# A fused attention-reading and expert kernel: the fourth batch's G is read inside its own unit, and raw second-layer weights are asked for in steps 10 to 12

## The chip, the core and the metric

The kernel runs on one core of one Trainium2 chip. The metric is the device time of one execution in microseconds, the median over runs. Engines are named as in the profile: PE is TensorE's matrix multiplication, PEld its weight load, DVE is VectorE, ACT is ScalarE, POOL is GpSimd, and SP is the engine that here only issues DMAs.

## The reference

```python
# x: B=4, H=8, S=512, D=64;  state: B, H, Ns=32, D
xread = softmax(scale * x @ state.T) @ state          # B,H,512,64
sread = softmax(scale * state @ x.T) @ x              # B,H,32,64
t = concat([xread, sread], axis=2) -> tokens 2176 x 512

P = exp(t @ w_gate - max)                             # 2176 x 8 experts
8 times: P /= row sums; P /= column sums; P *= N / E
y = sum over e of P[:, e] * (relu(t @ w1[e]) @ w2[e]) # w1 512x1024, w2 1024x512

h = y @ w_in                                          # 512 x 2048
out = (h * sigmoid(h)) @ w_out                        # 2048 x 512
```

## The kernel before

Every fp32 product is made of three fp32r products. A tile is split into a high part (a copy rounded to fp32r) and a low part (the rest), and `mm3` (L83 to L86) issues low times high on L84, high times low on L85 and high times high on L86.

The first expert layer is not computed from the tokens as they are. A token's xread is a mixture `a` of rows of `state`, so t @ w1 is a @ (state · w1), and the product of state and w1, called G, is made once per unit for all four batches. A unit is one half of one expert's hidden width: 8 experts times 2 halves are 16 units, u = 0 to 15. The G of a unit is computed one unit ahead in two pieces (`g_pieces`, matmuls pg on L441, ACT's copies and DVE's subtractions into `stg`), written to a DRAM tile `g_d` (L448) and read back batch by batch by `load_g(u, b)`, four DMAs on L475 each, in the layout the matmuls want.

A unit is 16 steps, k = 4 b + f: four batches b of 512 tokens, and four chunks f of 128 hidden columns. In a step PE runs S1 of the step that lies two ahead (6 matmuls into the bank `ph`; then ACT's relu `hh` on L512 and DVE's low part `hl` on L513), and then S2 of the step itself (12 matmuls into four banks `po`, with the step's `hh`, `hl` as one operand and the second-layer weights of chunk f, `h_w` and `l_w`, as the other). At a batch's last chunk DVE adds P times the four banks to `acc` (L567). PE keeps the order in which the code is written. The order on the other engines and on SP's queue is set by a scheduler when the kernel is built, from the order of the code and its own estimate of when data comes; each engine then works through its list in that order.

A weight tile takes four steps. SP asks for the raw tile (L182, `raw_w` in the trace, `raw_w2_7_0` in the order for unit 7, chunk 0). ACT casts it to the high part (L190, `h_w`), DVE subtracts to get the low part (L89, `l_w`), and PE uses both. The raw tiles share a pool with the tag "raw", three buffers deep before. The w2 pool holds five split tiles, one more than a unit needs: so chunk 0 of the next unit has a free slot, and chunk f = 1, 2, 3 of it needs the slot that S2 of step 12 + f − 1 frees. S2 of the new unit needs chunk f at its own step f, five steps later.

The calls in the main loop that belong to the change: for most units `load_w1(u + 2, ·)` at steps 7 to 10, `load_g(u + 1, b)` at steps 8, 9, 11 and 14 (units 0 and 1: 12 to 15), `load_w2(u + 1, f)` at steps 12 to 15, after the calls of `load_g`. Between them `convert` prepares the weights of the second network (raw64, cv, cvo; DMAs of wi_d and wo_d issued by ACT). After the 16 units the second network runs with the same S1 and S2 over w_in and w_out; it uses the "raw" buffers for `gv` and the tag "e2" for `sg`. In the first unit, steps also carry pieces of the attention stage, in a table `early`: ahead of S2 its first list, behind S2 its second; `positions(b)` makes softmax weights (tile `e2`), `back(b)` works on from there.

Of the kernel before, what the change touches and what calls it, by code (L numbers as in the profile page):

```python
# [11 lines left out]
F32 = mybir.dt.float32  # L12
# [9 lines left out]
def fused_kernel(ctx: ExitStack, tc: tile.TileContext, x, state, w_gate, w1, w2, w_in, w_out, out):  # L22
# [18 lines left out]
    DM = H * D  # L41
    E, _, F = w1.shape
# [18 lines left out]
    stp = ctx.enter_context(tc.tile_pool(name="stp", bufs=4))  # L61
    accp = ctx.enter_context(tc.tile_pool(name="accp", bufs=4))
    wp = ctx.enter_context(tc.tile_pool(name="wp", bufs=5))
    rawp = ctx.enter_context(tc.tile_pool(name="rawp", bufs=3))
    hp_ = ctx.enter_context(tc.tile_pool(name="hp", bufs=4))
    srp = ctx.enter_context(tc.tile_pool(name="srp", bufs=1))
    att = ctx.enter_context(tc.tile_pool(name="att", bufs=5))
# [116 lines left out]
    def load_split(src_ap, shape, nm, tag, slots, engine=nc.vector):  # L184
        if nm not in raws:
            load_raw(src_ap, shape, nm)
        raw = raws.pop(nm)
        hi = wp.tile(shape, F32R, tag=tag + "h", name=f"h_{nm}", bufs=slots)
        lo = wp.tile(shape, F32R, tag=tag + "l", name=f"l_{nm}", bufs=slots)
        nc.scalar.copy(hi, raw)  # L190
        lo_of(lo, raw, hi, engine)
        return hi, lo
# [8 lines left out]
        else:  # L201
            w1t[u, hp] = load_split(src, [128, FU], f"w1_{u}_{hp}", "w1", 4, nc.gpsimd if u == 0 else nc.vector)

    def load_w2(u, f):
        e, fh = divmod(u, UPE)
        r0 = fh * FU + f * 128
        w2t[u, f] = load_split(w2[e, r0:r0 + 128, :], [128, DM], f"w2_{u}_{f}", "w2", 5)

# [118 lines left out]
    def positions(b, q):  # L329

        pq = pm(f"pq{b}_{q}")
        for r in range(R):
            nc.tensor.transpose(pq[:, r * 128:(r + 1) * 128], s1_of[b][:, r, q * 128:(q + 1) * 128], ident)
        e2 = e2_of[b, q] = att.tile([128, 512], F32, tag="e2", name=f"e2_{b}_{q}", bufs=4)
        nc.scalar.copy(e2, pq)
        m2 = sm.tile([128, 1], F32, tag="m2", name=f"m2_{b}_{q}")
        nc.vector.tensor_reduce(out=m2, in_=e2, axis=AX.X, op=ALU.max)
        nc.vector.tensor_scalar_mul(m2, m2, -scale)
        z2 = sm.tile([128, 1], F32, tag="z2", name=f"z2_{b}_{q}")
        nc.scalar.activation(out=e2, in_=e2, func=AF.Exp, scale=scale, bias=m2, accum_out=z2)  # L340
        nc.vector.tensor_scalar_add(z2, z2, 1e-9)
        nc.vector.reciprocal(out=z2, in_=z2)
        nc.vector.tensor_scalar_mul(e2, e2, z2)
# [135 lines left out]
    def sr_first(u):  # L479
        ps = p1(f"psr_{u}")  # L480
        for hp in range(KD):
            wh, wl = w1t[u, hp]
            mm3(ps, srh[:, hp], srl[:, hp], wh, wl, hp == 0, hp == KD - 1)
        t = att.tile([128, FU], F32, tag="e2", name=f"hs_{u}", bufs=4)
        nc.scalar.activation(out=t, in_=ps, func=AF.Relu)
        hS[u] = t

# [14 lines left out]
    def S1(u, b, f):  # L502
        ph = p1(f"ph{u}_{b}_{f}")
        if u < NU:
            gh, gl = G[u, b][:, :, 0], G[u, b][:, :, 1]
            ah, al = (t[:, b % 2] for t in aT[b // 2])
            fs = slice(f * 128, (f + 1) * 128)
            for q in range(2):
                mm3(ph, gh[:, q, fs], gl[:, q, fs], ah[:, q], al[:, q], q == 0, q == 1)
            hh = hp_.tile([128, 512], F32R, tag="hh", name=f"hh{u}_{b}_{f}")  # L510
            hl = hp_.tile([128, 512], F32R, tag="hl", name=f"hl{u}_{b}_{f}")
            nc.scalar.activation(out=hh, in_=ph, func=AF.Relu)  # L512
            last["dve"] = nc.vector.scalar_tensor_tensor(out=hl, in0=ph, scalar=0.0, in1=hh.bitcast(F32), op0=ALU.max, op1=ALU.subtract)  # L513
        else:
            wh, wl = wit[u - NU, f]
            n = 128 * len(chunks[b])
            for k in range(KD):
                xh, xl = x2[b, k]
                mm3(ph[:, :n], wh[:, k], wl[:, k], xh, xl, k == 0, k == KD - 1)
            sg = att.tile([128, 512], F32, tag="e2", name=f"sg{u}_{b}_{f}", bufs=4)  # L520
            nc.scalar.activation(out=sg[:, :n], in_=ph[:, :n], func=AF.Sigmoid)  # L521
            gv = rawp.tile([128, 512], F32, tag="raw", name=f"gv{u}_{b}_{f}")
            nc.vector.tensor_tensor(out=gv[:, :n], in0=ph[:, :n], in1=sg[:, :n], op=ALU.mult)  # L523
            hh = hp_.tile([128, 512], F32R, tag="hh", name=f"hh{u}_{b}_{f}")
            hl = hp_.tile([128, 512], F32R, tag="hl", name=f"hl{u}_{b}_{f}")
            nc.scalar.copy(hh[:, :n], gv[:, :n])
            lo_of(hl[:, :n], gv[:, :n], hh[:, :n])
        hT[u, b, f] = (hh, hl)
# [74 lines left out]
    def both(piece, b, *bank):  # L603
# [4 lines left out]
        -1: ([lambda: x_turn(2, 2, pm), lambda: x_turn(2, 3, pm)], []),  # L608
        0: (both(scores, 2, pm) + [lambda: slots(2, 1)], both(mixing, 1, pm)),
        1: (both(positions, 0), [lambda hp=hp: x_turn(3, hp, pm) for hp in range(KD)]),  # L610
        2: (both(positions, 1), both(back, 0) + both(scores, 3, pm) + [lambda: slots(3, 1), lambda: state_reads(0)]),
        3: (both(mixing, 2, pm), [lambda: g_first(1, 0)]),
        4: ([lambda: g_first(1, 1)], [lambda: g_first(1, 2)]),
        5: ([lambda: g_first(1, 3)], both(back, 1)),
# [58 lines left out]
    for i in range(-LAG, len(steps)):  # L673
# [19 lines left out]
        if u < NU:  # L693
            if 0 < u:
                if u == 1 and k == 2:
                    sr_first(1)
                if u == 1 and k == 4:
                    sr_turn(1)
                if k == 7:
                    sread_second(u)  # L700
                if u + 1 < NU:
                    if k == (11 if u == 1 else 6):
                        sr_first(u + 1)
                    if k == (13 if u == 1 else 9):
                        sr_turn(u + 1)
                if u + 1 >= NU and k < 4:
                    load_win(0, k)
                convert_some((u - 2) * B * NF + k + 5)
            for unit, hp in first.get(u, {}).get(k, ()):
                load_w1(unit, hp)  # L710
            at = 12 if u == 1 else 7
            if 1 <= u and u + 2 < NU and at <= k < at + 4:
                load_w1(u + 2, k - at)
            loads = (12, 13, 14, 15) if u <= 1 else (8, 9, 11, 14)
            if u + 1 < NU and k in loads:
                load_g(u + 1, loads.index(k))
            if k >= 12:
                load_w2(u + 1, k - 12) if u + 1 < NU else load_wout(0, k - 12)
            if u == NU - 1:
                if 6 <= k < 10:  # L720
                    turn(0, k - 6)
                if 10 <= k < 14:
                    turn(1, k - 10)
                if k >= 14:
                    turn(2, 2 * (k - 14))
                    turn(2, 2 * (k - 14) + 1)
        else:
            v = u - NU
            if v == 0 and k < 8:
                turn(3 + k // 4, k % 4)  # L730
            if v + 1 < NV:
                if b == 3 and f < 2:
                    load_win(v + 1, f)
                if b == 4:
                    if f < 2:
                        load_win(v + 1, f + 2)
                    load_wout(v + 1, f)
# [31 lines left out]
```

## Time and profile before

| | before |
|---|---|
| median of 3 runs | 1740.56 us (1738.30 to 1741.57) |
| profiled execution, its own time | 1744.39 us |
| span of the profiled execution | 1742.6 us |
| mean granted TensorE clock | 0.988 |
| PE busy | 1690.5 us, 97% of the span |
| PEld, DVE, ACT busy | 1396.2, 891.2, 492.3 us |

The time of an execution is a little longer than the span, which runs from its first to its last instruction. The profiled execution lies 3.83 us above the median of the runs. The granted clock is the share of TensorE's full rate (2.4 GHz) that it was given, so 0.50 means 1.2 GHz.

### The profile page before, as it was taken

Reading aid. Unit: us, or ns where it says so; the run is one execution under the profiler, and the core shown is the slowest. Engines: PE = TensorE matmul, PEld = TensorE weight load, DVE = VectorE, ACT = ScalarE, POOL = GpSimd, SP = SyncE. Lnnn points to the kernel's source line nnn. Section 1 sums busy time; section 2 is a strip of 40 time slices with the busy share of each in tenths; the row PEclk is TensorE's granted clock in tenths of the full one; section 3 lists DMA queues with packets and bytes.
Section 4 is the critical chain, followed back from the end, with each engine's and each line's share of the span. In section 5 each row is a group of like instructions: output and inputs, shape, how many; then the busy total and the mean of one; then the engine's idle time right before and its main releaser. Section 6 shows DMA issues by size and latency. Waiting matters only on the chain.

```text
span 1742.6 us, 20238 instructions
## 1 busy us (share of the span) xinstructions
PE 1690.5 (97%) x7868; PEld 1396.2 (80%) x7868; DVE 891.2 (51%) x1524; ACT 492.3 (28%) x891; POOL 12.6 (1%) x15
## 2 busy tenths in 40 slices
PE   8999999999999999999999999999999999999999
PEld 7878787877878787878778787878788888888888
DVE  7642575555555555565655655465434433433333
ACT  5642244222222222232322222232212322222222
POOL 1010000000000000000000000000000000000000
PEclk9989999999999999999999999999999999999999
DMA  7042376565745464655647465655540103020211
GB/s 170 19 150 70 96 201 199 132 205 146 195 160 164 138 176 165 167 185 136 206 145 206 139 167 171 170 183 125 169 109 7 43 1 97 1 97 1 85 49 55
DMA packets 107631, 222.07 MB, mean 127 GB/s; under 512 B 28560, under 2 KB 44944, under 8 KB 107536
## 3 DMA queue, kind: packets, MB, share of 16 engines
q1 hardware_dynamic: 101152, 201.76, 40.5%
q10 hardware_dynamic: 6384, 19.02, 2.8%
q8 instruction: 62, 1.02, 0.2%
q14 instruction: 33, 0.27, 0.0%
HBM read 136.59 MB, written 84.15 MB: 127 GB/s over the span
## 4 chain that ended last, share of the span: by engine, by line
PE 79%; DVE 2%; issue 1%; ACT 1%; ACTq 0%; DVEq 0%
PE po L85 16%; PE po L84 15%; PE po L86 15%; PE ph L86 9%; PE ph L84 9%; PE ph L85 9%; PE pg L441 3%; DVE acc L567 1%; PE psr L85 1%; PE psr L84 1%; PE psr L86 1%; DVE l_w L89 1%; ACT hh L512 1%; PE px L591 0%; DVE hl L513 0%
## 5 line engine op out<-in xcount | busy, mean ns | idle before, releaser
L84 PE MATMUL po<-h_w,hl 128*128 128x512 f32 x1024 | 410.4, 401 | 22.7 <-ACT h_w L190 22.7
L85 PE MATMUL po<-l_w,hh 128*128 128x512 f32 x1024 | 406.6, 397 | 14.1 <-DVE l_w L89 14.1
L86 PE MATMUL po<-h_w,hh 128*128 128x512 f32 x1024 | 404.0, 395 | 0.0
L513 DVE SCALAR_TENSOR_TENSOR hl<-ph,hh 128x512 fp32r<-128x512 f32 x256 | 176.7, 690 | 419.8 <-ACT hh L512 419.3
L512 ACT ACTIVATE hh<-ph 128x512 fp32r<-128x512 f32 x256 | 153.2, 598 | 666.0 <-PE ph L86 662.2
L84 PEld LDWEIGHTS po<-h_w,hl 128*128 128x128 f32 x1024 | 194.7, 190 | 79.6 <-ACT h_w L190 29.8
L85 PEld LDWEIGHTS po<-l_w,hh 128*128 128x128 f32 x1024 | 195.0, 190 | 61.3 <-DVE l_w L89 22.5
L86 PEld LDWEIGHTS po<-h_w,hh 128*128 128x128 f32 x1024 | 195.1, 191 | 40.8
L84 PE MATMUL ph<-aTh,G 128*128 128x512 f32 x512 | 203.5, 398 | 0.4 <-DVE hl L513 0.4
L86 PE MATMUL ph<-aTh,G 128*128 128x512 f32 x512 | 200.2, 391 | 0.0
L85 PE MATMUL ph<-aTl,G 128*128 128x512 f32 x512 | 200.2, 391 | 0.0
L567 DVE SCALAR_TENSOR_TENSOR acc<-po,P,acc 128x512 f32<-128x512 f32 x224 | 153.1, 742 | 6.6 <-PE po L86 6.6
L523 DVE TENSOR_TENSOR gv<-ph,sg 128x384 f32<-128x384 f32 (+1 forms) x80 | 48.9, 611 | 191.2 <-ACT sg L521 191.2
L84 PE MATMUL ph<-x2h,wil 128*128 128x384 f32 (+1 forms) x320 | 115.4, 361 | 0.0
L86 PE MATMUL ph<-x2h,wih 128*128 128x384 f32 (+1 forms) x320 | 114.7, 358 | 0.0
L85 PE MATMUL ph<-x2l,wih 128*128 128x384 f32 (+1 forms) x320 | 114.4, 357 | 0.0
L86 PEld LDWEIGHTS ph<-aTh,G 128*128 128x128 f32 x512 | 96.5, 189 | 20.6
L84 PEld LDWEIGHTS ph<-aTh,G 128*128 128x128 f32 x512 | 96.9, 189 | 19.8 <-DVE hl L513 0.6
L85 PEld LDWEIGHTS ph<-aTl,G 128*128 128x128 f32 x512 | 96.8, 189 | 19.1
L86 PE MATMUL po<-woh,hh 128*128 128x512 f32 x272 | 106.8, 393 | 0.0
L85 PE MATMUL po<-wol,hh 128*128 128x512 f32 x272 | 106.7, 392 | 0.0
L84 PE MATMUL po<-woh,hl 128*128 128x512 f32 x272 | 105.8, 389 | 0.0
(163 smaller groups left out, 1848.9 us busy)
## 6 DMA issues: line engine op xcount, KB each, us to landing
g_d<-stg SPq DMA_DIRECT2D x120, 512.0 KB, 4.0
G<-g_d SPq DMA_DIRECT2D x240, 256.0 KB, 5.5
raw_w<-in_moe_w_dram SPq DMA_DIRECT2D x136, 256.0 KB, 5.3
raw<-in_moe_w_in_dram SPq DMA_DIRECT2D x16, 512.0 KB, 6.2
wi_d<-cvo ACTq DMA_DIRECT2D x16, 512.0 KB, 2.7
raw<-in_moe_w_out_dram SPq DMA_DIRECT2D x16, 512.0 KB, 6.3
wo_d<-cvo ACTq DMA_DIRECT2D x16, 512.0 KB, 3.1
x<-in_x_dram SPq DMA_DIRECT2D x16, 256.0 KB, 4.9
```

The lines of the kernel that those rows point to most:

```text
L84: nc.tensor.matmul(ps, al, bh, start=first, stop=False)
L85: nc.tensor.matmul(ps, ah, bl, start=False, stop=False)
L86: nc.tensor.matmul(ps, ah, bh, start=False, stop=last)
L89: engine.tensor_tensor(out=lo, in0=src, in1=hi.bitcast(F32), op=ALU.subtract)
L441: nc.tensor.matmul(pg[hp, half], a[lanes[half], hp], w[lanes[half]], start=i == 0, stop=i == 2)
L512: nc.scalar.activation(out=hh, in_=ph, func=AF.Relu)
L513: last["dve"] = nc.vector.scalar_tensor_tensor(out=hl, in0=ph, scalar=0.0, in1=hh.bitcast(F32), op0=ALU.max, op1=ALU.subtract)
L523: nc.vector.tensor_tensor(out=gv[:, :n], in0=ph[:, :n], in1=sg[:, :n], op=ALU.mult)
L567: nc.vector.scalar_tensor_tensor(out=a, in0=ps, scalar=P[:, t, e:e + 1], in1=a, op0=ALU.mult, op1=ALU.add)
```

## The change

The raw pool gets a fourth buffer, and the tag "e2" has three in place of four. `load_w2` can ask for the raw tile alone. For units 1 to 14 the raw tiles of the next unit's w2 are asked for in step 10 (chunk 0), 11 (chunks 1 and 2) and 12 (chunk 3); the cast and the subtraction are still called in steps 12 to 15, and now ahead of the calls for w1 and G. The read of G's fourth batch moves out of the unit before into step 0 of the unit that uses it, and the third batch's from step 11 to step 12 (unit 0 and 1: from 14 to 15). In step 2 of the first unit `back(0)` and `positions(1)` change places.

```diff
-    rawp = ctx.enter_context(tc.tile_pool(name="rawp", bufs=3))
+    rawp = ctx.enter_context(tc.tile_pool(name="rawp", bufs=4))
...
-    def load_w2(u, f):
+    def load_w2(u, f, only_raw=False):
...
+        if only_raw:
+            load_raw(w2[e, r0:r0 + 128, :], [128, DM], f"w2_{u}_{f}")
+        else:
+            w2t[u, f] = load_split(w2[e, r0:r0 + 128, :], [128, DM], f"w2_{u}_{f}", "w2", 5)
...
# e2, hs and sg, all with the tag "e2":  bufs=4  ->  bufs=3
...
-        2: (both(positions, 1), both(back, 0) + both(scores, 3, pm) + [lambda: slots(3, 1), lambda: state_reads(0)]),
+        2: (both(back, 0), both(positions, 1) + both(scores, 3, pm) + [lambda: slots(3, 1), lambda: state_reads(0)]),
...
+            if k >= 12:
+                load_w2(u + 1, k - 12) if u + 1 < NU else load_wout(0, k - 12)
             for unit, hp in first.get(u, {}).get(k, ()):
                 load_w1(unit, hp)
             at = 12 if u == 1 else 7
             if 1 <= u and u + 2 < NU and at <= k < at + 4:
                 load_w1(u + 2, k - at)
-            loads = (12, 13, 14, 15) if u <= 1 else (8, 9, 11, 14)
+
+            if u and k == 0:
+                load_g(u, 3)
+            for f in ({10: (0,), 11: (1, 2), 12: (3,)}.get(k, ()) if 1 <= u and u + 1 < NU else ()):
+                load_w2(u + 1, f, True)
+            loads = (12, 13, 15) if u <= 1 else (8, 9, 12)
             if u + 1 < NU and k in loads:
                 load_g(u + 1, loads.index(k))
-            if k >= 12:
-                load_w2(u + 1, k - 12) if u + 1 < NU else load_wout(0, k - 12)
```

What the scheduler makes of it is seen best where unit 7 follows unit 6; the other boundaries look alike. ACT's list before, from the first cast of unit 7's w2 (`h_w2_7_f`) on; `hh7_0_2` is the relu of unit 7, batch 0, chunk 2, and `ph7_0_2` its bank:

```order
L190 CAST h_w2_7_0_5358<-raw_w2_7_0_5356 128x512
L512 ACTIVATE hh7_0_2_5472<-ph7_0_2_5465 128x512
L190 CAST h_w2_7_1_5389<-raw_w2_7_1_5387 128x512
L244 DMA wo_d1_167<-cvo_13_5456 128x1024
L512 ACTIVATE hh7_0_3_5500<-ph7_0_3_5493 128x512
L446 CAST stg8_0_0_5527<-pg8_0_0_5511 128x512
L446 CAST stg8_0_1_5531<-pg8_0_1_5512 128x512
L446 CAST stg8_1_0_5535<-pg8_1_0_5519 128x512
L446 CAST stg8_1_1_5539<-pg8_1_1_5520 128x512
L512 ACTIVATE hh7_1_0_5562<-ph7_1_0_5555 128x512
L190 CAST h_w2_7_2_5424<-raw_w2_7_2_5422 128x512
L190 CAST h_w2_7_3_5461<-raw_w2_7_3_5459 128x512
```

The same place in ACT's list after, from the relu of unit 6's batch 3, chunk 2 on:

```order
L515 ACTIVATE hh6_3_2_5336<-ph6_3_2_5329 128x512
L190 CAST h_w2_7_0_5357<-raw_w2_7_0_5295 128x512
L190 CAST h_w2_7_1_5393<-raw_w2_7_1_5325 128x512
L515 ACTIVATE hh6_3_3_5375<-ph6_3_3_5368 128x512
L244 CAST cvo_13_5453<-cv_13_5287 128x512
L190 CAST h_w2_7_2_5421<-raw_w2_7_2_5327 128x512
L515 ACTIVATE hh7_0_0_5404<-ph7_0_0_5397 128x512
L190 CAST h_w2_7_3_5456<-raw_w2_7_3_5361 128x512
L515 ACTIVATE hh7_0_1_5432<-ph7_0_1_5425 128x512
L515 ACTIVATE hh7_0_2_5467<-ph7_0_2_5460 128x512
L247 DMA wo_d1_167<-cvo_13_5453 128x1024
L515 ACTIVATE hh7_0_3_5500<-ph7_0_3_5493 128x512
```

The casts of chunks 0 and 1 move from behind `hh7_0_1` and `hh7_0_2` to behind `hh6_3_2`, three and four relus earlier, and those of chunks 2 and 3 from behind `hh7_1_0` to behind `cvo_13` and `hh7_0_0`, five and four relus earlier. DVE's subtractions `l_w2_7_f` go with them: chunk 0's stands behind the four `acc` additions of unit 6's last batch before, and ahead of them after.

SP's queue before, from the read of G's first batch for unit 7 on (x4 are the four DMAs of one `load_g`):

```order
L475 DMA G_7_0_5209<-g_d7_4902 32x2x1024 x4
L475 DMA G_7_1_5255<-g_d7_4902 32x2x1024 x4
L223 DMA raw64_13_5285<-in_moe2_w_out_dram 128x1024
L182 DMA raw_w1_8_3_5289<-in_moe_w1_dram 128x512
L475 DMA G_7_2_5323<-g_d7_4902 32x2x1024 x4
L182 DMA raw_w2_7_0_5356<-in_moe_w2_dram 128x512
L182 DMA raw_w2_7_1_5387<-in_moe_w2_dram 128x512
L475 DMA G_7_3_5417<-g_d7_4902 32x2x1024 x4
L182 DMA raw_w2_7_2_5422<-in_moe_w2_dram 128x512
L182 DMA raw_w2_7_3_5459<-in_moe_w2_dram 128x512
L448 DMA g_d8_5510<-stg8_0_0_5527 128x1024
L448 DMA g_d8_5510<-stg8_0_1_5531 128x1024
```

SP's queue after, from the same place on:

```order
L478 DMA G_7_0_5209<-g_d7_4902 32x2x1024 x4
L478 DMA G_7_1_5255<-g_d7_4902 32x2x1024 x4
L226 DMA raw64_13_5285<-in_moe2_w_out_dram 128x1024
L182 DMA raw_w2_7_0_5295<-in_moe_w2_dram 128x512
L182 DMA raw_w2_7_1_5325<-in_moe_w2_dram 128x512
L182 DMA raw_w2_7_2_5327<-in_moe_w2_dram 128x512
L182 DMA raw_w2_7_3_5361<-in_moe_w2_dram 128x512
L478 DMA G_7_2_5363<-g_d7_4902 32x2x1024 x4
L478 DMA G_7_3_5488<-g_d7_4902 32x2x1024 x4
L451 DMA g_d8_5510<-stg8_0_0_5527 128x1024
L451 DMA g_d8_5510<-stg8_0_1_5531 128x1024
```

The four raw tiles of w2 now stand together ahead of the reads of `G_7_2` and `G_7_3`, and `raw_w1_8_3` has moved up out of this piece; before, `raw_w2_7_2` and `raw_w2_7_3` were queued behind `G_7_3`.

## Rows read from the trace of the kernel before

**Rows 1.** The page, part 1: busy time of each engine, its share, instructions.

```profile
PE 1690.5 (97%) x7868; PEld 1396.2 (80%) x7868; DVE 891.2 (51%) x1524; ACT 492.3 (28%) x891; POOL 12.6 (1%) x15
```

**Rows 2.** Waits of TensorE, whole span: total us, times, longest.

```profile
PE po L84 <- ACT h_w L190: 22.7, 17, 3.1
PE po L85 <- DVE l_w L89: 14.1, 22, 1.5
...
PE pq L333 <- DVE aTl L89: 1.2, 1, 1.2
```

**Rows 3.** Timeline of TensorE: the first boundary wait of all, unit 1.

```profile
184.48 0.49 PE L84 MATMUL po<-h_w,hl 128*128 128x512 f32 x1 [1.08 <-ACT h_w L190]
```

**Rows 4.** Timeline of TensorE: the last boundary wait, unit 14.

```profile
1226.37 0.50 PE L85 MATMUL po<-l_w,hh 128*128 128x512 f32 x1 [0.32 <-DVE l_w L89]
```

**Rows 5.** Timeline of TensorE where unit 7 begins.

```profile
662.47 0.39 PE L84 MATMUL po<-h_w,hl 128*128 128x512 f32 x1
663.86 0.50 PE L85 MATMUL po<-l_w,hh 128*128 128x512 f32 x1 [1.00 <-DVE l_w L89]
664.20 0.40 PE L86 MATMUL po<-h_w,hh 128*128 128x512 f32 x1
```

**Rows 6.** Timeline of TensorE, third step of unit 7.

```profile
675.26 0.49 PE L84 MATMUL po<-h_w,hl 128*128 128x512 f32 x1 [1.25 <-ACT h_w L190]
```

**Rows 7.** Timeline of ScalarE around the same boundary.

```profile
658.65 0.60 ACT L512 ACTIVATE hh<-ph 128x512 fp32r<-128x512 f32 x1 [3.48 <-PE ph L86]
659.14 0.61 ACT L190 CAST h_w<-raw_w 128x512 fp32r<-128x512 f32 x1
...
674.11 0.60 ACT L512 ACTIVATE hh<-ph 128x512 fp32r<-128x512 f32 x1 [1.76 <-PE ph L86]
674.60 1.13 ACT L190 CAST h_w<-raw_w 128x512 fp32r<-128x512 f32 x2
```

**Rows 8.** Timeline of VectorE around the same boundary.

```profile
659.28 0.69 DVE L513 SCALAR_TENSOR_TENSOR hl<-ph,hh 128x512 fp32r<-128x512 f32 x1 [3.06 <-ACT hh L512]
659.89 2.71 DVE L567 SCALAR_TENSOR_TENSOR acc<-po,P,acc 128x512 f32<-128x512 f32 x4
...
663.12 0.68 DVE L89 TENSOR_TENSOR l_w<-raw_w,h_w 128x512 fp32r<-128x512 f32 x1
```

**Rows 9.** Timeline of SP's queue ahead of unit 7 (rows may join issues).

```profile
642.92 0.83 SPq L182 DMA_DIRECT2D raw_w<-in_moe_w_dram  x2
650.42 1.74 SPq L475 DMA_DIRECT2D G<-g_d  x4
652.26 11.93 SPq L182 DMA_DIRECT2D raw_w<-in_moe_w_dram  x2
```

**Rows 10.** The tile raw_w, 620 to 670 us: issue to landing.

```profile
DMA to landing us min/median/max: 2.6/2.7/9.4
```

**Rows 11.** Five half-clock stretches: length, busy by engine, clock, DMA share, GB/s.

```profile
593.99:600.82 6.83, 6.16 (x15) 4.81 (x16) 1.21 (x3) 0.00 (x0) 0.00 (x0) 0.50 0.86 273
...
sum 20.48, PE 19.53 PEld 15.06 DVE 6.13 ACT 1.19 POOL 0.00; mean PE 3.91 PEld 3.01 DVE 1.23 ACT 0.24 POOL 0.00
```

**Rows 12.** Timeline of TensorE within the half-clock stretch of 593.99.

```profile
596.10 0.63 PE L85 MATMUL po<-l_w,hh 128*128 128x512 f32 x1
596.53 0.63 PE L86 MATMUL po<-h_w,hh 128*128 128x512 f32 x1
```

**Rows 13.** Timeline of ScalarE where unit 15 follows unit 14.

```profile
1277.88 0.62 ACT L190 CAST h_w<-raw_w 128x512 fp32r<-128x512 f32 x1 [2.12 <-PE po L86]
1279.24 0.60 ACT L512 ACTIVATE hh<-ph 128x512 fp32r<-128x512 f32 x1 [0.74 <-DVE l_w L89]
```

**Rows 14.** Timeline of TensorE at that place.

```profile
1279.04 0.39 PE L84 MATMUL po<-h_w,hl 128*128 128x512 f32 x1
...
1281.53 0.39 PE L86 MATMUL po<-h_w,hh 128*128 128x512 f32 x1
```

**Rows 15.** The page, part 6: DMA issues, KB each, median us to landing.

```profile
G<-g_d SPq DMA_DIRECT2D x240, 256.0 KB, 5.5
```

More of the change, by code (lines that the diff above doesn't have):

```diff
@@ L202, in load_w1 @@
             w1t[u, hp] = load_split(src, [128, FU], f"w1_{u}_{hp}", "w1", 4, nc.gpsimd if u == 0 else nc.vector)
-    def load_w2(u, f):
+    def load_w2(u, f, only_raw=False):
         e, fh = divmod(u, UPE)
         r0 = fh * FU + f * 128
-        w2t[u, f] = load_split(w2[e, r0:r0 + 128, :], [128, DM], f"w2_{u}_{f}", "w2", 5)
+        if only_raw:
+            load_raw(w2[e, r0:r0 + 128, :], [128, DM], f"w2_{u}_{f}")
+        else:
+            w2t[u, f] = load_split(w2[e, r0:r0 + 128, :], [128, DM], f"w2_{u}_{f}", "w2", 5)
     wi_d = [dram.tile([KD, 128, 2, FU], F32, name=f"wi_d{v}") for v in range(NV)]
@@ L333, in positions @@
             nc.tensor.transpose(pq[:, r * 128:(r + 1) * 128], s1_of[b][:, r, q * 128:(q + 1) * 128], ident)
-        e2 = e2_of[b, q] = att.tile([128, 512], F32, tag="e2", name=f"e2_{b}_{q}", bufs=4)
+        e2 = e2_of[b, q] = att.tile([128, 512], F32, tag="e2", name=f"e2_{b}_{q}", bufs=3)
         nc.scalar.copy(e2, pq)
@@ L483, in sr_first @@
             mm3(ps, srh[:, hp], srl[:, hp], wh, wl, hp == 0, hp == KD - 1)
-        t = att.tile([128, FU], F32, tag="e2", name=f"hs_{u}", bufs=4)
+        t = att.tile([128, FU], F32, tag="e2", name=f"hs_{u}", bufs=3)
         nc.scalar.activation(out=t, in_=ps, func=AF.Relu)
@@ L519, in S1 @@
                 mm3(ph[:, :n], wh[:, k], wl[:, k], xh, xl, k == 0, k == KD - 1)
-            sg = att.tile([128, 512], F32, tag="e2", name=f"sg{u}_{b}_{f}", bufs=4)
+            sg = att.tile([128, 512], F32, tag="e2", name=f"sg{u}_{b}_{f}", bufs=3)
             nc.scalar.activation(out=sg[:, :n], in_=ph[:, :n], func=AF.Sigmoid)
```

## The prediction

> **What bounds the kernel now.** I read the page's busy shares first: PE is busy for 1690.5 us, 97% of the span [rows 1]. Nothing that leaves PE's instructions as they are can win more than PE's idle time and what PE does slowly, so the next view is that of PE's waits. Two of its rows hold nearly all of the idle time after the first stage: PE waits 17 times for `h_w` (22.7 us) and 22 times for `l_w` (14.1 us), 36.8 us in 39 waits [rows 2]. In the timeline they lie between 184.48 and 1226.37 us [rows 3, 4], every one where a unit begins, at each of the units 1 to 14. So the thing to explain is one boundary, and whether its cause goes.
>
> I take the one to unit 7. PE has the high part of chunk 0 at 662.47 but waits 1.00 us for its low part [rows 5]. Of chunk 2 it lacks the high part and waits 1.25 us [rows 6]. The raw data is not the cause: SP asks for chunks 0 and 1 at 642.92 and for chunk 2 at 652.26 [rows 9], and landing takes 2.7 us in the median and 9.4 at most [rows 10], so by 661.7 chunk 2 is there, 13 us before its cast. The cause is the place in the lists. ACT casts chunk 0 only behind the relu of 658.65, though a slot is free, and chunks 2 and 3 behind the relu of 674.11 [rows 7], which itself comes from the S1 directly ahead of the S2 that wants the weights. DVE then does chunk 0's subtraction behind the `hl` of 659.28 and four additions to `acc`, and ends 3.4 us after the cast [rows 7, 8]. The read of `G_7_3` at 650.42 also holds up SP: raw chunks 2 and 3 are queued behind it [rows 9], which is a reason for the scheduler to expect them late.
>
> **What the waits cost beyond themselves.** Where nothing waits, matmuls start every 0.226 us (1279.04 to 1281.53 in 11 steps) [rows 14]. From 662.47 to 664.20 two steps take 1.73 us where 0.45 would do, so a wait of 1.00 costs 1.28 us: 0.28 more than the view of waits says [rows 5]. I give that to each of the 39: 10.9 us. Third, there are five stretches at half clock (granted 0.50, that is 1.2 GHz), all right behind boundary waits, 20.48 us with 19.53 us of PE at work [rows 11]. There a matmul starts every 0.43 us [rows 12], so 1 − 0.226 / 0.43 = 0.474 of that work, 9.3 us, is lost. By the Trainium skill (TensorE: Matmul & The Clock Gate, section Terms) the penalty is the throttled time times one minus the granted share, 20.48 × 0.5 = 10.2 us, by which the saving below would be 57.9 us. The trace's cadence decides, and the sum goes by 9.3.
>
> **The change part by part.** *Raw tiles of w2 asked for in steps 10 to 12, load_w2 called ahead of w1 and G, fourth raw buffer.* No instruction is added on PE, ACT or DVE. In the order after, the casts of unit 7 stand three to five relus earlier and the subtractions go with them, chunk 0's ahead of the four additions. A step is 18 matmuls, 4.08 us. Chunk 0 is then cast behind the relu at about 658.65 − 3 × 4.08 = 646.4, some 16 us before PE wants it. Chunks 1 to 3 each wait for their slot, and get it from the S2 five steps ahead of their own: from its end some 17 us remain for a cast of 0.61 and a subtraction of 0.69 us. The kernel before has this pattern once: at unit 15 the cast waits 2.12 us for PE, ends at 1278.50, and the relu behind it starts at 1279.24, in its usual place after S1 [rows 13], while PE runs on without a wait [rows 14]. So I take all three parts at the full size:
>
> 36.8 + 10.9 + 9.3 = 57.0 us, 4.1 us for each of the 14 boundaries.
>
> *The read of the fourth batch's G at step 0 of its own unit, the third's one step later.* The same DMAs, later. Batch 3's first S1 runs at step 10 of the unit, some 40 us behind the call, and a read takes 5.5 us to land [rows 15]. In SP's order `G_7_3` stands directly behind `G_7_2`, and waits for the same S1 as before, so it leaves near 650 as it does now [rows 9]. Cost: nothing, covered by 35 us; with that cover gone PE would stand still for up to 5.5 us at each of 15 units, 82 us.
>
> *Tag "e2" with three buffers.* `sg` is read by the next DVE operation and then free; PE has no wait after 1226.37 [rows 4], so nothing there leans on a fourth buffer. Taken at nothing. *Step 2 of unit 0.* `positions(1)` and `back(0)` change places; the largest wait of PE for such a piece is 1.2 us [rows 2]. It may go or come twice: between −1.2 and +1.2, and I take 0.
>
> **The sum.** The profiled execution would go from 1744.39 to 1687.4 us. It lies 3.83 us above the median of the runs, so the median would be 1740.56 − 57.0 = 1683.6. I leave 2 us for waits that stay, at unit 1 above all, where the calls keep steps 12 to 15 in the unit before and the casts have the least room. Forecast: 1686 us.
>
> **The rivals.**
>
> *The clock stays.* Only two of the parts return and the stretches at half clock remain, for another reason than the waits: in the one of 593.99 the DMA engines are busy at 0.86 [rows 11], so it could be them. Against it: five of the 14 boundaries have such a stretch and no place without waits has one in this part. Time: 1740.56 − 36.8 − 10.9 = 1692.9.
>
> *Half of the boundaries keep their waits*, because the raw tiles, now all behind one another, come late there or the scheduler finds no earlier place. The order speaks against it, since I find the casts moved two to five steps at each of the 14 boundaries. Time: 1740.6 − 28.5 = 1712.
>
> *The change doesn't do what it says.* The casts stand earlier in the lists, but wait there, and PE gets its weights no sooner. They would have to be some 16 us late for that. Time: about 1740.
>
> *Slower: early casts hold up the relus.* ACT works through its list in order, so a cast that waits for a raw tile holds the relus behind it, and with them `hh`, `hl` and PE. By the Trainium skill (PSUM — Partial Sum Buffer, section Engine vs sequencer instructions) the queues of ScalarE and VectorE are strictly first in, first out, which speaks against putting a cast further ahead. The trace agrees: at 1279.24 the relu starts only after the cast of 1277.88 [rows 13]. Its price: S1 writes a bank again two steps, 8.16 us, later; from S1's first matmul to the end of `hl` some 2.8 us pass (six matmuls of 0.226, then 0.60 and 0.69 [rows 7, 8]). So a relu may be 5.3 us late for nothing; each us more costs 1 us at each boundary, and the kernel becomes slower once a raw tile is some 5.3 + 4.1 = 9.4 us late at all 14. At 12 us it would be 14 × 6.7 − 57 = 37 us slower, 1777. Against it: in SP's order the four raw tiles stand ahead of `G_7_2`, whose read waits for an S1 four steps ahead of `G_7_3`'s 650.42. Even if they left only then, at 634, and took the longest landing, 9.4 us [rows 10], they would be there at 643.5, 3 us before the relu of 646.4.
>
> **How the numbers follow.** A measurement of this kernel can't tell 0.2%, 3.5 us, from no change. All three parts return: 0.74 (1680 to 1690). The clock stays: 0.10. Half of the boundaries: 0.08. No change: 0.04. Slower: 0.04. The range for 8 in 10 begins at 1678, which is the sum without the 2 us left over, less 1.2 us for step 2 and the spread of the three runs shown; it reaches up past the clock's case to 1704, where five of the boundaries keep their 4.1 us. Faster 0.92, same 0.04, slower 0.04.
>
> **What would show it.** Right: in the view of PE's waits the rows for `h_w` and `l_w` fall from 36.8 us to under 4; the mean granted clock rises from 0.988, with 0.50 only before 184 us; on ACT the casts of a unit's w2 stand behind the relus of the last batch before it, with idle time released by PE's `po`. PE's busy time would fall by what the half clock cost. The raw tiles of w2 would land before the relu that their cast follows. Wrong: waits of ACT for DMAs of `raw_w` with relus late behind them and new waits of PE for `hl`; waits of PE for `G`; or half-clock stretches where PE has no wait ahead.

## The result

| | before | changed |
|---|---|---|
| median of the first series | 1739.70 us (4 runs, 1738.30 to 1741.57) | 1680.14 us (4 runs, 1679.99 to 1690.46) |
| profiled execution, its own time | 1744.39 us | 1679.99 us |
| its span, mean granted clock | 1742.6 us, 0.988 | 1678.2 us, 1.000 |
| pooled median | 1740.10 us (36 runs beside the experiments, 1735.92 to 1747.85) | 1683.22 us (14 runs: these 4, and 10 of two later series, 1679.99 to 1690.46) |

The changed kernel is faster: the ratio is 0.9672, with a 95% interval from 0.9634 to 0.9710; the forecast of 1686 us stands at 0.969 of the first median before. Two later series, told below, gave 0.9680 both times, at 1683.18 and 1684.94 us. One more run of before, at 4316.87 us and a granted clock of 1.000, is far outside all the others and is left out of every number here.

In the page of the profile PE's busy share goes from the 97% of [rows 1] to 99%. Engine, busy us, share of the span and instructions:

```profile
PE 1660.0 (99%) x7868; PEld 1383.1 (82%) x7868; DVE 893.7 (53%) x1524; ACT 493.4 (29%) x891; POOL 12.7 (1%) x15
```

PE has the same 7868 instructions. In the view of PE's waits from 170 to 1228 us, where 39 waits for `h_w` and `l_w` took 36.8 us [rows 2], neither is left. Two other waits stand there now; such waits took 0.2 us before. In total, times, longest:

```profile
PE pc L420 <- DVE cs L417: 1.1, 1, 1.1
PE pg L444 <- DVE hl L516: 0.9, 1, 0.9
```

Unit 7 now begins at 625.48 us. TensorE's timeline there, against [rows 5]: start, us, operation.

```profile
625.48 0.39 PE L84 MATMUL po<-h_w,hl 128*128 128x512 f32 x1
625.71 0.39 PE L85 MATMUL po<-l_w,hh 128*128 128x512 f32 x1
625.94 0.39 PE L86 MATMUL po<-h_w,hh 128*128 128x512 f32 x1
```

Start follows start after 0.23 us. The same boundary on ScalarE, against [rows 7]; in brackets the idle time ahead of an instruction and what ended it:

```profile
609.42 0.60 ACT L515 ACTIVATE hh<-ph 128x512 fp32r<-128x512 f32 x1 [3.54 <-PE ph L86]
609.92 0.61 ACT L190 CAST h_w<-raw_w 128x512 fp32r<-128x512 f32 x1
612.08 0.62 ACT L190 CAST h_w<-raw_w 128x512 fp32r<-128x512 f32 x1 [1.55 <-PE po L86]
613.50 0.60 ACT L515 ACTIVATE hh<-ph 128x512 fp32r<-128x512 f32 x1 [0.80 <-PE ph L86]
616.18 0.62 ACT L244 CAST cvo<-cv 128x512 fp32r<-128x512 f32 x1 [2.08 <-DVE cv L238]
616.71 0.61 ACT L190 CAST h_w<-raw_w 128x512 fp32r<-128x512 f32 x1
617.58 0.60 ACT L515 ACTIVATE hh<-ph 128x512 fp32r<-128x512 f32 x1 [0.26 <-PE ph L86]
620.24 0.62 ACT L190 CAST h_w<-raw_w 128x512 fp32r<-128x512 f32 x1 [2.06 <-PE po L86]
621.66 0.60 ACT L515 ACTIVATE hh<-ph 128x512 fp32r<-128x512 f32 x1 [0.80 <-PE ph L86]
```

The four casts of unit 7's w2 start at 609.92, 612.08, 616.71 and 620.24, all before the unit begins. Two of them wait for PE's `po`, that is for their slot, and not for data (the prediction had such a wait for three of them); the relus of 613.50 and 621.66 behind them still wait for PE. VectorE's list there, against [rows 8]:

```profile
620.90 0.69 DVE L89 TENSOR_TENSOR l_w<-raw_w,h_w 128x512 fp32r<-128x512 f32 x1 [1.66 <-ACT h_w L190]
622.29 0.69 DVE L516 SCALAR_TENSOR_TENSOR hl<-ph,hh 128x512 fp32r<-128x512 f32 x1 [0.70 <-ACT hh L515]
622.90 2.71 DVE L570 SCALAR_TENSOR_TENSOR acc<-po,P,acc 128x512 f32<-128x512 f32 x4
```

The last subtraction of the four runs ahead of the `acc` additions of 622.90. And SP's queue, against [rows 9], where two raw tiles of w2 left at 642.92 and the others between 652.26 and 664.19; now all four leave together, ahead of the next read of G:

```profile
587.64 4.12 SPq L182 DMA_DIRECT2D raw_w<-in_moe_w_dram  x4
596.62 9.58 SPq L478 DMA_DIRECT2D G<-g_d  x2
```

### The profile page after: what moved, and what is told of

It is laid out like the page before. It is cut to its first block, busy times and chain, and to the rows that moved or that the text cites. A ratio compares the mean times of both kernels' runs of the same rounds, so it can differ in the third digit from the quotient of the medians.

```text
span 1678.2 us, 20174 instructions
## 1 busy us (share of the span) xinstructions
PE 1660.0 (99%) x7868; PEld 1383.1 (82%) x7868; DVE 893.7 (53%) x1524; ACT 493.4 (29%) x891; POOL 12.7 (1%) x15
## 4 chain that ended last, share of the span: by engine, by line
PE 84%; DVE 0%; issue 0%
PE po L84 17%; PE po L85 16%; PE po L86 16%; PE ph L84 10%; PE ph L86 10%; PE ph L85 10%; PE pg L444 3%; PE psr L85 1%; PE psr L84 1%; PE psr L86 1%; PE px L594 0%; PE pt L495 0%; DVE acc L566 0%; DVE l_w L89 0%; DVE accs L566 0%; DVE hl L516 0%
## 5 line engine op out<-in xcount | busy, mean ns | idle before, releaser
L84 PE MATMUL po<-h_w,hl 128*128 128x512 f32 x1024 | 404.2, 395 | 0.0
L86 PE MATMUL po<-h_w,hh 128*128 128x512 f32 x1024 | 398.9, 390 | 0.0
L85 PE MATMUL po<-l_w,hh 128*128 128x512 f32 x1024 | 398.8, 389 | 0.0
L84 PEld LDWEIGHTS po<-h_w,hl 128*128 128x128 f32 x1024 | 192.2, 188 | 49.4 <-issue 10.9
L89 DVE TENSOR_TENSOR l_w<-raw_w,h_w 128x512 fp32r<-128x512 f32 x128 | 87.1, 690 | 61.5 <-ACT h_w L190 60.8
L524 ACT ACTIVATE sg<-ph 128x384 f32<-128x384 f32 (+1 forms) x80 | 42.8, 535 | 220.2 <-PE ph L86 217.6
```

Of the source, the lines that this page charges most:

```text
L84: nc.tensor.matmul(ps, al, bh, start=first, stop=False)
L85: nc.tensor.matmul(ps, ah, bl, start=False, stop=False)
L86: nc.tensor.matmul(ps, ah, bh, start=False, stop=last)
L89: engine.tensor_tensor(out=lo, in0=src, in1=hi.bitcast(F32), op=ALU.subtract)
```

## Where the time came from: the granted clock read run by run

The 36 runs of the kernel before differ by 12 us, the 14 of the changed one by 10, and each run's time goes with its mean granted clock. The runs of before at 0.993 take 1735.9 to 1736.8 us, those at 0.986 take 1747.2 to 1747.9. The changed kernel's runs at 1.000 take 1680.0 to 1680.2 us, those at 0.997 take 1683.0 to 1683.5, those at 0.994 take 1689.6 and 1690.5. A straight line through either set (least squares) gives 1724.8 us plus 1.60 us for each thousandth of clock that is missing before, and 1679.6 us plus 1.52 us after, with standard errors of 0.5 and 0.4 us on the two times at full clock. No run of before stands above 0.993, so its 1724.8 us lies beyond its runs. The slope agrees with the cadences of [rows 12, 14]: a thousandth is 3.4 us at half clock, of which 0.474 is lost, 1.6 us.

So the gain has two parts. At full clock the two kernels differ by 1724.8 − 1679.6 = 45.2 us: the waits that went and what follows each of them, less the two waits that came. The rest is clock: the median run of before stands at 0.990 to 0.992, that of the changed kernel at 0.996 to 1.000, series by series.

## The experiments

Medians, with the lowest and highest run, the clocks of the runs and the ratio to the runs of before in the same series:

| run | median us | runs, range | granted clock | ratio [95%] |
|---|---|---|---|---|
| e1_half | 1710.53 | 6, 1707.89 to 1717.41 | 0.988 to 0.995 | 0.9837 [0.9813, 0.9861] |
| e2_only_g | 1699.51 | 5, 1698.92 to 1705.30 | 0.992 to 0.996 | 0.9765 [0.9742, 0.9788] |
| e3_only_e2 | 1741.83 | 12, 1739.07 to 1745.52 | 0.987 to 0.992 | 1.0008 [0.9994, 1.0021] |
| e4_no_raw | 1687.91 | 5, 1682.88 to 1691.26 | 0.994 to 0.999 | 0.9692 [0.9667, 0.9716] |
| e5_after_again | 1683.18 | 4, 1682.99 to 1683.53 | 0.997 to 0.998 | 0.9680 [0.9662, 0.9698] |
| e6_g_order | 1688.09 | 4, 1683.22 to 1689.66 | 0.995 to 0.999 | 0.9703 [0.9682, 0.9725] |
| e7_raw3 | 1687.24 | 5, 1682.17 to 1689.23 | 0.993 to 0.998 | 0.9696 [0.9674, 0.9718] |
| e8_no_g | 1680.29 | 5, 1679.73 to 1687.18 | 0.995 to 1.000 | 0.9672 [0.9649, 0.9696] |
| e9_raw2 | 1691.97 | 6, 1690.27 to 1698.05 | 0.991 to 0.995 | 0.9726 [0.9700, 0.9751] |
| e10_raw1 | 1718.50 | 4, 1716.25 to 1721.07 | 0.987 to 0.990 | 0.9872 [0.9843, 0.9901] |
| e11_sr_late | 1679.91 | 5, 1678.70 to 1681.61 | 0.998 to 1.000 | 0.9651 [0.9626, 0.9675] |
| e12_after_third | 1684.94 | 6, 1680.18 to 1689.57 | 0.994 to 1.000 | 0.9680 [0.9651, 0.9708] |

The theory under test, called the order theory in the expectations, is the prediction's: the gain is made boundary by boundary, by the place of the casts in ACT's and DVE's lists. Its rivals: the raw tiles' supply (buffers and early requests) makes it; early casts hold up the relus. Not run alone were the order of the calls and the early requests.

**The change for half of the units.** The conditions of the main loop get a bound, so that units 8 to 14 keep the code order of before:

```diff
-            if k >= 12:
-                load_w2(u + 1, k - 12) if u + 1 < NU else load_wout(0, k - 12)
+            if k >= 12 and u < 7:
+                load_w2(u + 1, k - 12)
...
-            if u and k == 0:
+            if 0 < u < 8 and k == 0:
                 load_g(u, 3)
-  ... if 1 <= u and u + 1 < NU else ()):
+  ... if 1 <= u < 7 else ()):
                 load_w2(u + 1, f, True)
-            loads = (12, 13, 15) if u <= 1 else (8, 9, 12)
+            loads = (12, 13, 15) if u <= 1 else (8, 9, 12) if u < 7 else (8, 9, 11, 14)
...
                 load_g(u + 1, loads.index(k))
+            if k >= 12 and u >= 7:
+                load_w2(u + 1, k - 12) if u + 1 < NU else load_wout(0, k - 12)
```

> The whole change for the units up to 7 and the order of before for units 8 to 14 (buffers and step 2 as in the changed kernel). Order theory (what is won is won boundary by boundary, by the place of the casts in the lists): units 8 to 14 keep their waits, in the trace of before 23 us with refill and one half-clock stretch, so about 1680 + 23 = 1703 us; PE waits for h_w and l_w only after 740 us. Rival, the gain lies in the buffers and the early stage: 1680 to 1686 us, or near 1740.

PE's waits from 170 to 1228 us in its trace:

```profile
PE po L84 <- ACT h_w L190: 11.7, 8, 3.1
PE po L85 <- DVE l_w L89: 3.7, 9, 0.9
```

They are 17 waits of 15.4 us, the first ending at 717 us, and PE has none of them up to unit 7. The time is 7 us above the expected one, which had counted one stretch at half clock, and the clock accounts for that: the fastest run is at 0.995, and 1.55 us for each missing thousandth leave 1700 us at full clock. The changed kernel's 1679.6 with 15.4 us of waits and 17 × 0.28 us behind them is 1699.8. In its profile four stretches at half clock lie among the units that wait, each behind a wait. The changed units before them have none, though the first unit has one of 6.8 us at 119.8 us. First and last of the four, then the time from 200 to 700 us:

```profile
717.17:720.58 3.41, 3.35 (x8) 2.29 (x9) 1.10 (x2) 0.30 (x1) 0.00 (x0) 0.50 0.98 297
...
1113.11:1116.53 3.42, 3.42 (x9) 2.63 (x9) 0.31 (x1) 0.00 (x0) 0.00 (x0) 0.50 1.03 323
200.00:700.00 500.00, 499.11 (x2268) 407.90 (x2267) 302.44 (x524) 147.26 (x259) 0.00 (x0) 1.00 0.61 180
```

**G's move alone.**

```diff
+            if u and k == 0:
+                load_g(u, 3)
-            loads = (12, 13, 14, 15) if u <= 1 else (8, 9, 11, 14)
+            loads = (12, 13, 15) if u <= 1 else (8, 9, 12)
```

> Only G's fourth batch is read in its own unit, the third's one step later; nothing else changes. In the order the casts of chunk 2 then stand two or three relus earlier, those of chunk 0 stay one relu ahead of their use. Order theory: the pairs of waits for chunk 2 (about 2.1 us a boundary, 30 us) go, those for chunk 0's low part (1.0 to 1.3 us a boundary) stay: 1702 to 1712 us. Supply theory (the raw tiles' early request and the fourth buffer make the gain): no change, 1736 to 1742 us.

This edit, to which the prediction gave no gain, brings 40 us by itself, some 32 of them work and the rest clock (with 1.55 us for each missing thousandth, its runs stand near 1692.5 us at full clock, against 1724.8 before):

```profile
PE po L85 <- DVE l_w L89: 7.0, 9, 1.0
PE po L84 <- ACT h_w L190: 3.8, 3, 1.3
```

12 waits are left of 39: three pairs, of a wait for a high and one for a low part, and six single waits for chunk 0's low part. The other pairs, nearly all chunk 2's, are gone. The time lies 2.5 us under the expected range, because I had counted a wait for chunk 0's low part at each of the 14 boundaries, and before it stands alone at six of them. PE had not waited for G's DMAs; the read of `G_7_3` stood in SP's queue ahead of raw chunk 2. With it behind, chunk 2 of unit 7 leaves 6.4 us after chunk 0 in place of 9.3, and the scheduler puts its cast directly behind chunk 1's, the x2 below (SP's queue, then ScalarE):

```profile
623.29 6.75 SPq L182 DMA_DIRECT2D raw_w<-in_moe_w_dram  x3
```

```profile
642.83 0.60 ACT L512 ACTIVATE hh<-ph 128x512 fp32r<-128x512 f32 x1 [2.98 <-PE ph L86]
643.33 1.13 ACT L190 CAST h_w<-raw_w 128x512 fp32r<-128x512 f32 x2
```

The supply theory, which expected no change, falls in that form.

**Three e2 buffers and the exchange in step 2 alone.**

```diff
-        2: (both(positions, 1), both(back, 0) + both(scores
+        2: (both(back, 0), both(positions, 1) + both(scores
...
# tag "e2": bufs=4 -> bufs=3
```

> Only three e2 buffers and the exchange in step 2. Prediction's step: within 1.2 us of before, 1738 to 1742 us. Rival, the exchange is what takes the half-clock stretches at 102 and 119 to 136 us away: about 9 us faster, 1731 us, and full clock there in the trace. If those stretches come and go from run to run, single runs of this kernel will spread by about 10 us and their mean granted clock with them.

No change, as the prediction's step had it: the interval holds 1, and PE's two waits are those of before to the tenth (22.7 us in 17, 14.1 us in 22). The exchange doesn't lift the clock either.

**Without the early requests.** The two lines that call `load_w2(u + 1, f, True)` are taken out of the changed kernel.

> The changed kernel without the early requests for raw tiles of w2 in steps 10 to 12; the fourth buffer, the order of the calls and G's move stay. In the order the casts still stand two to four relus ahead of their use at nearly all boundaries (unit 3's chunk 1 directly behind the relu). Order theory: within 4 us of the changed kernel, 1680 to 1684 us. Supply theory: half of the gain or more is lost, 1705 us or above, and ACT waits for DMAs of raw_w.

```profile
PE po L84 <- ACT h_w L190: 1.3, 1, 1.3
...
PE po L85 <- DVE l_w L89: 0.3, 1, 0.3
```

One boundary, unit 3, has its pair of waits back, 1.6 us, as the order said. The median lies 4 us above the expected range, and the rest of the difference is clock: the fastest run, at 0.999, takes 1682.88 us. So the early requests are worth about 2 us here, and are not what makes the gain.

**The changed kernel again, G's move with the order of the calls, three raw buffers, and G as before.** e5 has no edit. The other three:

```diff
# e6_g_order: before, with
+            if k >= 12:
+                load_w2(u + 1, k - 12) if u + 1 < NU else load_wout(0, k - 12)
             for unit, hp in first.get(u, {}).get(k, ()):
...
+            if u and k == 0:
+                load_g(u, 3)
...
# e7_raw3: changed, with
-    rawp = ctx.enter_context(tc.tile_pool(name="rawp", bufs=4))
+    rawp = ctx.enter_context(tc.tile_pool(name="rawp", bufs=3))
...
# e8_no_g: changed, with
-            if u and k == 0:
-                load_g(u, 3)
-            loads = (12, 13, 15) if u <= 1 else (8, 9, 12)
+            loads = (12, 13, 14, 15) if u <= 1 else (8, 9, 11, 14)
```

> The changed kernel once more, for the clock of each run. If the stretches at half clock come by the run: most runs near 1680 us at a mean granted clock of 1.000, some 3 to 12 us above it at 0.994 to 0.999, each thousandth of the clock less costing about 1.6 us (0.001 of 1680 us is 3.4 us at half clock, and 0.47 of that is lost). If a run is slower at a clock of 1.000, something else is in play.

> G's move and the calls of load_w2 ahead of those for w1 and G; three raw buffers, four e2 buffers, step 2 and all requests as before. In the order chunk 0's casts stand four relus ahead of their use, chunk 1's one, chunks 2 and 3 two and three; only unit 3's chunk 1 stands directly behind the relu. Order theory: all waits but about 2 us at unit 3 go, 1682 to 1690 us. Supply theory: with three raw buffers the tiles come late, ACT waits for them, and half of the gain or more is lost: 1705 us or above.

> The changed kernel with three raw buffers in place of four. Its casts stand as early as in the changed kernel. Order theory: within 4 us of the changed kernel. Rival, early casts hold up the relus: with a raw buffer less the tiles of w2 can be late, ACT waits for DMAs of raw_w, relus start late and PE waits for hl: 5 us to 30 us above the changed kernel.

> The changed kernel with G read as before (third batch at step 11, fourth at step 14 of the unit before). Order theory: the casts stand two to five relus ahead all the same, so within 4 us of the changed kernel. If G's move is what frees SP's queue for the raw tiles, waits for h_w come back: 1690 us or above.

All four runs of e5 stand at 0.997 or 0.998, where I had expected most at 1.000, and lie within 1.2 us of the line. All three variants have at most one boundary with a wait for weights left; e6 has unit 3's, as expected. Their medians lie between 1680 and 1688 us, and their clocks spread as widely: at 0.998 to 1.000 they take 1682 (e7), 1683 (e6, at 0.999) and 1680 us (e8). e7 and e8 lie near the changed kernel's line in the fit above, e6 about 2 us above it, which its pair of waits costs. e6 is the strongest: with three raw buffers, all requests as before, and only the order of the calls and the read of G changed, nearly the whole gain is there. Whether a variant makes a fall of the clock likelier than the changed kernel can't be told from four or five runs.

**Two raw buffers and one.** The changed kernel with `bufs=2`, and with `bufs=1` (then `gv` of the second network gets its own two buffers).

```diff
-    rawp = ctx.enter_context(tc.tile_pool(name="rawp", bufs=4))
+    rawp = ctx.enter_context(tc.tile_pool(name="rawp", bufs=1))
...
-            gv = rawp.tile([128, 512], F32, tag="raw", name=f"gv{u}_{b}_{f}")
+            gv = rawp.tile([128, 512], F32, tag="gv", name=f"gv{u}_{b}_{f}", bufs=2)
```

> The changed kernel with two raw buffers in place of four. The casts keep their early places in the order, two to five relus ahead of their use, but a raw tile can only be asked for when the second one before it has been subtracted, so they wait longer for data. Order theory with the tolerance of the prediction (a relu may be 5.3 us late for nothing): ACT waits for raw_w by 10 to 40 us in all, PE hardly; 1680 to 1692 us, as the clock goes. Rival, early casts hold up the relus: PE waits for hl, 1695 us or above.

> The changed kernel with one raw buffer (gv of the second network gets two buffers of its own, so that only the weight tiles of the experts are tight). Each raw tile now waits for the subtraction of the one before it and then for its transfer, 3 to 9 us; the casts stand one to three relus ahead of their use, at some boundaries chunk 3 directly behind the relu. Here the rival (casts that wait for data hold up the relus behind them) must show if it exists: single waits of ACT for raw_w above 5.3 us, and PE waiting for hl behind them; 1695 to 1760 us. If relus can be held up longer for nothing, only the chunk 3 stalls come back, about 2 us at three boundaries: 1685 to 1695 us.

Here the casts do wait for data. With two buffers, ScalarE where unit 2 begins, and ahead of unit 4:

```profile
249.37 0.62 ACT L190 CAST h_w<-raw_w 128x512 fp32r<-128x512 f32 x1 [5.06 <-DMA raw_w<-in_moe_w_dram]
249.90 0.59 ACT L515 ACTIVATE hh<-ph 128x512 fp32r<-128x512 f32 x1
```

```profile
402.78 0.60 ACT L515 ACTIVATE hh<-ph 128x512 fp32r<-128x512 f32 x1 [2.40 <-PE ph L86]
...
407.42 0.62 ACT L190 CAST h_w<-raw_w 128x512 fp32r<-128x512 f32 x1 [0.56 <-DMA raw_w<-in_moe_w_dram]
407.94 0.59 ACT L515 ACTIVATE hh<-ph 128x512 fp32r<-128x512 f32 x1
410.70 0.62 ACT L190 CAST h_w<-raw_w 128x512 fp32r<-128x512 f32 x1 [2.17 <-DMA raw_w<-in_moe_w_dram]
411.23 0.59 ACT L515 ACTIVATE hh<-ph 128x512 fp32r<-128x512 f32 x1
```

At 249.37 the cast of a weight tile waits 5.06 us for its DMA, and the relu behind it starts with no idle time: it is held up. DVE's subtraction waits 4.80 us for the cast too, with its work on P and on `acc` queued behind, and PE then waits 1.96 us for an addition to `acc`:

```profile
250.03 0.69 DVE L89 TENSOR_TENSOR l_w<-raw_w,h_w 128x512 fp32r<-128x512 f32 x1 [4.80 <-ACT h_w L190]
```

```profile
255.85 0.50 PE L84 MATMUL po<-h_w,hl 128*128 128x512 f32 x1 [1.96 <-DVE acc L566]
```

That is the prediction's slower rival at work in one place, by a longer way: through DVE's list and an addition to `acc`, where the rival had `hh` and `hl`. At 407.94 and 411.23 relus are held up too, the first 1.1 us behind its time (402.78 and a step of 4.08 make 406.86), and PE doesn't wait; from 310 us on its view of waits is empty. So at these relus lateness of about 1 us was free, and 5 us with other work behind it wasn't; the 5.3 us that I worked out for a relu alone was not reached in a step without such work, and stays untested. The trace of two buffers lies 10.5 us behind the changed kernel's, all of it lost before unit 3 begins (335.60 against 324.82 us). About 8 of them are clock: three stretches at half clock, at 19.6, 122.0 and 265.4 us, are 17.1 us long together. All six runs stand at 0.991 to 0.995; whether the buffers do that isn't shown.

With one buffer the supply is short everywhere:

```profile
ACT h_w L190 <- DMA raw_w<-in_moe_w_dram: 75.5, 45, 4.1
```

```profile
PE psr L84 <- ACT h_w L190: 10.0, 2, 7.2
PE po L84 <- ACT h_w L190: 3.8, 3, 1.3
```

ACT waits 45 times for raw tiles, PE loses most to the w1 weights of `psr`, and 38 us of the gain are gone. Of these, 27 are lost before unit 3 begins, at 352.09 us, and some 17 are clock, by the line above at its 0.989. The time lies in the range that I gave the rival, but the rival's signs don't appear: no wait of ACT for a raw tile is above 4.1 us, and PE has no wait for `hl` in S2. At three boundaries chunk 3 has its waits back, as expected.

**The wait ahead of the half-clock stretch at 119 us.** In the changed kernel a piece of the first unit moves behind the next S1:

```diff
-        9: (both(positions, 3), [lambda: state_reads(2)]),
-        10: ([lambda: logits(0)], both(back, 3)),
+        9: (both(positions, 3), []),
+        10: ([lambda: state_reads(2), lambda: logits(0)], both(back, 3)),
```

> The changed kernel, and in the first unit state_reads(2) runs in step 10 behind S1 in place of the end of step 9, where PE waits 1.67 us for a bank. The wait falls below 0.5 us: about 1.3 us faster. If the half-clock stretch at 119.6 us of other runs comes from that wait, it goes too: no stretch there, and most runs at 1677 to 1680 us with a clock of 0.999 or 1.000. If it has another cause, runs at 0.994 to 0.998 stay as common as in the changed kernel.

> The changed kernel beside the run before it: 1680 to 1690 us as its clock goes, with 1680 at 1.000 and 1683 at 0.997.

The changed kernel has the same wait in each of its three traces, 1.7 us for `psr` at 118 to 120 us, and behind it the clock falls in some runs and not in others. Two stretches of e5, then the same two of the first trace: busy us of each engine, clock, DMA share, GB/s.

```profile
116.40:119.60 3.20, 1.53 (x14) 1.41 (x13) 3.13 (x5) 2.36 (x5) 1.79 (x2) 1.00 0.58 232
119.60:126.40 6.80, 6.80 (x28) 6.31 (x28) 0.60 (x3) 0.52 (x2) 1.16 (x1) 0.50 1.03 314
```

```profile
116.40:119.60 3.20, 1.57 (x14) 1.57 (x15) 3.01 (x5) 2.21 (x5) 1.95 (x2) 1.00 0.63 251
119.60:126.40 6.80, 6.80 (x49) 6.28 (x49) 1.46 (x4) 1.30 (x4) 1.01 (x1) 1.00 1.04 314
```

PE works 1.53 and 1.57 of the 3.20 us ahead, and the DMA engines are fully busy in both 6.80 us; one trace has 0.50 behind it, the other 1.00. With the piece moved, PE works 2.70 of the same 3.20 us:

```profile
116.40:119.60 3.20, 2.70 (x15) 2.00 (x14) 3.13 (x6) 3.20 (x7) 1.25 (x2) 1.00 0.40 160
119.60:126.40 6.80, 6.80 (x53) 6.45 (x53) 1.96 (x5) 0.92 (x4) 1.71 (x2) 1.00 1.03 329
```

The wait there is 0.50 us now, all five runs stand at 0.998 to 1.000, and the median is 1679.91 us against 1684.94 in the same series for the changed kernel, 0.3% less. By the changed kernel's line about 1 us of the 5 is work, as expected, and the rest clock. The changed kernel's own first series had 1680.14, so that this version is faster is not shown.

## Why the prediction was right

**What bounds the kernel.** Right: 36.8 us of waits at 14 boundaries were there to be won, and all went. The half change shows that they are won boundary by boundary.

**The cause of the waits.** Right: not the landing of the raw tiles but the place of the casts. The proof is e6, which takes neither buffers nor early requests, and e4. The sum put all 57.0 us on one bundle, early requests, order of the calls and fourth buffer; of it the requests turned out to be worth 2 us (e4) and the buffer none that shows (e7). One reading was off: by [rows 7, 8] DVE's subtraction starts 3.4 us after the cast's end and ends 4.05 us after it. In the changed kernel's own trace unit 7's raw tiles, four of them leaving together, take longer to land than the median of [rows 10], the last also longer than the 9.4 us that the prediction took as the longest, and PE waits for none:

```profile
DMA to landing us min/median/max: 9.0/9.2/9.7
```

**The three terms.** The sum was 57.0 us. Over all runs the medians differ by 1740.10 − 1683.22 = 56.9 us, and in the first series by 59.6. That close an agreement is luck: two misses cancel. Waits and refill were given 36.8 + 10.9 = 47.7 us, and at full clock the kernels differ by 45.2; the clock was given 9.3 us, and is worth about 11.7. The first miss is not in what a wait costs beyond itself. From the start of unit 4 to that of unit 5 before, with three waits and no half clock between, then the same in the changed kernel, where PE has none:

```profile
421.61 0.39 PE L84 MATMUL po<-h_w,hl 128*128 128x512 f32 x1
500.26 0.39 PE L84 MATMUL po<-h_w,hl 128*128 128x512 f32 x1
```

```profile
399.98 0.39 PE L84 MATMUL po<-h_w,hl 128*128 128x512 f32 x1
475.14 0.39 PE L84 MATMUL po<-h_w,hl 128*128 128x512 f32 x1
```

The unit takes 78.65 us before and 75.16 after. The waits are 1.00, 1.25 and 0.32 us, so 0.92 us lie beyond them, 0.31 each, against the 0.28 of the prediction. Most of what the sum lacked are the two new waits of the changed kernel, for `cs` and `hl`, 2.0 us with 0.2 of the kind before.

PE's busy time fell by 30.5 us, where the prediction had it fall by what the half clock cost. The refill stands in that time too, since the view counts PE as busy while its matmuls start late behind a wait: 9.3 at the boundaries, 10.9 of refill and 8.7 in the first unit, told next, make 28.9.

**The clock's term was mis-sized by its scope.** I counted "five stretches at half clock, all right behind boundary waits". The trace of before has two more in the first unit, at 102.47 and from 119.54 to 136.61 us, 20.5 us long together, and I left them out because the change doesn't touch that place (length, busy us by engine, clock):

```profile
102.47:105.89 3.42, 3.42 (x12) 2.28 (x12) 1.38 (x8) 1.17 (x8) 0.00 (x0) 0.50 0.00 0
119.54:136.61 17.07, 17.07 (x64) 15.22 (x64) 2.19 (x5) 1.30 (x4) 1.86 (x2) 0.50 1.04 276
```

The first trace of the changed kernel has neither, though the prediction's sign of being right allowed for 0.50 there, and is 8.7 us ahead already where unit 0 ends (a matmul at 169.93 us before stands at 161.26); that is why trace against trace 64.4 us went and not 57. In other runs of the changed kernel a part of them is back: 6.8 us at 119.6 in e5, and in e12 this one at 120.8 and the other too:

```profile
103.72:107.13 3.41, 3.41 (x14) 2.22 (x15) 1.38 (x8) 1.07 (x6) 0.00 (x0) 0.50 0.00 0
```

Ahead of the one at 103.72, as ahead of that at 102.47 before, PE has no wait above 0.2 us in the 30 us before it. By the prediction's list, half clock where PE has no wait ahead is a sign of being wrong. In the first unit that sign is there; at the boundaries it is not. The forecast of 1686 lies within the runs, which go from 1680 to 1690 with the clock; the first series' 1680.14 is the case in which it stayed up.

By the rule of the Trainium skill that the prediction cited (TensorE: Matmul & The Clock Gate, section Terms), half of the throttled time is the penalty at half clock, an estimate of 1.7 us for each thousandth of clock on a 1680 us span. The runs give less: 1.52 after and 1.60 before.

**The G part.** "Cost: nothing" was right within the whole change: without it, e8, the time is the same, and in the changed kernel PE waits for no read of G. That it brings nothing was not right for the part alone: e2 wins 40 us. The prediction had named the reason, raw chunks 2 and 3 queued behind `G_7_3`, and gave it no price. The parts of this change overlap: G's move alone, or the calls' order with G's move, or requests and order without G's move, each lead the scheduler to earlier casts, and what the first one wins the others can't win again.

**2 us left for unit 1.** No wait for weights is left at any boundary, so they were not needed for what they were meant for. The two new waits in units 1 and 2 take about as much.

**The rivals.** *The clock stays*: wrong in the boundaries, where no half-clock stretch is left. The DMA engines alone are not the cause: at 119.6 us they are busy at 1.03 in the trace at half clock and at 1.04 in the one at full clock. *Half of the boundaries* and *no change*: no trace of them. *Early casts hold up the relus*: something near it exists, at two raw buffers, but in the changed kernel the four tiles of unit 7 leave at 587.64 to 591.4 us and are there by about 601, 9 us ahead of the first cast. The row that the prediction took for it, the relu of 1279.24 [rows 13], can't show it, as ACT stood idle for 0.74 us between that cast and the relu; the relu of 249.90 in e9, which starts behind its cast without idle time, does.

## What to carry to other kernels

When an engine waits for a converted weight, look at when the raw data landed before giving it more buffers or earlier requests: here it had been there for 13 us, and the cast stood too far back in a list that a scheduler had ordered. The order of the calls and the place of one read moved it, without a buffer or an early request. And where a kernel's runs spread by half a percent, set each run's time against its granted clock: a line through them separates what a change took out of the program from what the clock did in that run, and one profiled execution can stand on either side.

## What the hardware showed that I had not expected

Behind the same wait of 1.7 us the same program ran at the 1.2 GHz level for 6.8 us in one execution (e5) and at 2.4 GHz in another (the first trace); so it is not settled by the program alone. At the boundaries every stretch at half clock began in a wait of PE or right behind one, in the traces of before, e1, e3, e6, e9 and e10. In the first unit this does not hold: the stretches at 102.47 us before and at 103.72 in e12 have no such wait ahead. With the wait at 118 us made shorter, five runs stood at 0.998 or more, where six runs of the changed kernel beside them went down to 0.994; that the wait did it is likely by these eleven runs, but not shown. Why one execution falls and another doesn't stays open.
